# A fused attention and gated-MLP kernel: in its first pair of batches, the first layer one tile ahead and the weight sums rearranged

## The chip, the cores and the metric

The kernel runs on one core of one Trainium2 chip. Its time is device microseconds, the median of three runs. A core has a tensor engine (PE, with its weight loads as PEld), a vector engine (DVE), a scalar engine (ACT), GpSimd (POOL), and a sync engine (SP) that here only issues DMA transfers. Every engine runs its own queue strictly in order. Semaphores tie the queues together.

## The reference, cut to what matters

```python
scores = scale * x @ state^T;  a = softmax(scores);   xread = a @ state     # 512 tokens per head
scores2 = scale * state @ x^T; a2 = softmax(scores2); sread = a2 @ x        # 32 states per head
x = concat([xread, sread])           # (8 batches, 544 rows) -> 4352 rows of 512
h = x @ w_in                         # 512 -> 2048
g = h * cos(h)
out = g @ w_out                      # 2048 -> 512
```

`w_in` and `w_out` come in as float64 and are turned into float32 on the chip by integer operations. The rest is float32.

## The kernel before, in words

**Tiles and steps.** For one batch the gated layer is a grid of 16 tiles of 128 features by 512 tokens. One loop runs over `all_tiles`: a step is a tile, 16 steps are a batch, 32 (`PERIOD`) are a pair of batches; the state rows' tiles come last. Steps 0 to 27 are emitted by `first_pair`, all later ones by `later_pair`. From step 32 on tiles go two by two.

**What a tile goes through.** `hidden` (L489) is the first layer: four matmuls into a PSUM bank. `gate` (L559) on ACT rounds h to integers, `gate2` (L562) on DVE takes the difference, `gate3` (L565) on ACT is the sine, `gate4` (L579) on DVE multiplies and stores g in `g_all`. In the first pair the banks for h are two, so `hidden` of a tile waits for `gate4` of the tile two before.

**What else is in a step.** Each step of a batch has lists made by `plan`, one for each engine and place: `go(0)` is PE's work (token transposes, scores, `products`, which fold the state into `w_in`), `go(1)` ACT's copies of it ahead of `gate3`, `go(3)` DVE's part ahead of `gate4`, `go(2)`, `go(4)` and `go(5)` what comes after. Until step 16 a step also converts one block of the weights: passes 1 and 2 on ACT (L243, L246), b and c on DVE (L249, L252), the integer add d on POOL (L257). `inverse` (L383, L384) is the reciprocal of the softmax sums. At its end a step runs `first_product` or `second_product` (L632), the plain product with a11 and a12.

**The fast products.** Apart from those two, the products with `w_out` are done as seven smaller ones of an outer 2 x 2 scheme, and each of the seven again as seven stages of an inner one (`Product`, stages at L744, from step 29 on). That needs sums of weights. `weight_sum` (L1093) makes the outer sums, `inner_weights` (L670) the inner ones into four `TEMPS` and then sends eight blocks to DRAM (L672), from where `fetch_block` (L682) brings a block for each stage. `Product.sums` and `outer_sum` (both L691) are differences of g. `halves` (L508), `sw_sums` (L522) and `seven_part` (L539) do the same for the first layer from batch 2 on.

**What sets the order.** All is written out by hand. Tables tell at which step a thing is put into the queues (`weights_at`, `outer_at`, `sums_at`, `stage_at`), and memory for g is a list `quads_free` of numbered quads of `g_all`: `gate4` and `sums` take the first, and a user appends its quad when its last reader has been queued. The order in this list decides which later writer waits for which earlier reader. Quads 5 to 8 first hold `w_out` (A11, A12, A21, A22), 9 to 11 raw weights, and 4 is `TEMPS`.

Of the kernel before, what the change touches and what calls it, by code (L numbers as in the profile page):

```python
# [22 lines left out]
def kernel(  # L23
# [240 lines left out]
    class Attention:  # L264
# [117 lines left out]
        def inverse(self, v):  # L382
            nc.vector.tensor_scalar(v, v, 1e-9, None, op0=ALU.add)  # L383
            nc.vector.reciprocal(v, v)  # L384

        def sums(self):
            self.reduce1([self.z1[:, j] for j in range(2)], ALU.add)
            self.inverse(self.m1 if self.b == 0 else self.i12)

# [125 lines left out]

    def sw_sums(t, engine):
        (b11, b12, b21, b22), swS = weights_of(t)
        t1, t2, t4 = [swS[:, i] for i in range(3)]
        sub = ALU.subtract
        for o, x1, x2, op in ((t1, b21, b22, ALU.add), (t2, t1, b11, sub),  # L520
                              (t4, b12, t2, sub), (b21, b11, b21, sub)):
            engine.tensor_tensor(o, x1, x2, op=op)  # L522

# [136 lines left out]

    def inner_weights(which, m, engine=None):

        m11, m12, m21, m22 = quarters(m)
        t1, t2, t3, t4 = [quad(TEMPS)[:, n].rearrange("p (i d) -> p i d", d=P)
                          for n in range(4)]
        for o, x1, x2, op in ((t1, m21, m22, ALU.add),
                              (t2, t1, m11, ALU.subtract),
                              (t3, m11, m21, ALU.subtract),
                              (t4, m12, t2, ALU.subtract)):
            (engine or nc.gpsimd).tensor_tensor(o, x1, x2, op=op)  # L670
        for n, block in enumerate((m11, m12, t4, m22, t1, t2, t3, m21)):
            nc.sync.dma_start(  # L672
                out=blocks_kept[which, n].rearrange("p (i d) -> p i d", d=P),
                in_=block)
# [19 lines left out]
    class Product:  # L694
# [17 lines left out]
        def sums(self, k):  # L712
            lo, hi = self.quads()
            engine = nc.gpsimd
            if k == 1:
                self.q1 = quads_free.pop(0)
                self.t1 = quad(self.q1)[:, :, LO]
                self.t2 = quad(self.q1)[:, :, HI]
                sub(engine, self.t1, lo[:, :, HI], lo[:, :, LO])
            elif k == 2:  # L720
                sub(engine, self.t2, hi[:, :, HI], self.t1)
            elif k == 3:
                self.t3 = lo[:, :, HI]
                if not self.in_place:
                    self.q3 = quads_free.pop(0)
                    self.t3 = quad(self.q3)[:, :, LO]
                sub(engine, self.t3, hi[:, :, HI], lo[:, :, HI])
            else:
                sub(engine, self.t1, hi[:, :, LO], self.t2)

        def stage(self, k, copy):
# [19 lines left out]
            elif k == 2:  # L751
                nc.vector.tensor_tensor(u2, c[:, LO], t5, op=ALU.add)
                self.sums(4)
            elif k == 3:
                copy(b[:, HI], u2)  # L755
            elif k == 4:
                nc.vector.tensor_tensor(c[:, HI], c[:, LO], t5, op=ALU.add)
            elif k == 5:
                self.out(0, b)
                if self.frees:  # L760
                    quads_free.extend(quads_of[self.row][1:])
            elif k == 6:
                self.out(1, c)
                quads_free.append(self.q1)
                if not self.in_place:
                    quads_free.append(self.q3)
                if self.frees:
                    quads_free.append(quads_of[self.row][0])

# [187 lines left out]
    def plan(b):  # L957
# [3 lines left out]
        def prod(s, b, nt, *bank):  # L961
            pe[s].append((b, "products", nt) + bank)
            if b == 1 and 0 < nt < 3:
                x_dve[s].append((b, "products_taken", nt) + bank)
            else:
                x_act[s].append((b, "products_kept", nt) + bank)

# [45 lines left out]
        if b == 0:  # L1013
            pe[0].append((0, "products", 0, SIDE, HC, WC))
            y_dve[0] += [(0, "products_taken", 0, SIDE, HC, WC),
                         (0, "inverse2")]
            prod(7, 0, 2, SIDE)
            prod(11, 0, 3)
            prod(13, 1, 0, SIDE)
# [52 lines left out]
    for n in range(B // 2):  # L1072
        end = n == B // 2 - 1
        for r, engine, o, x1, x2, half in (
                ((25, 26), dve, 0, 2, 0, 0), ((27, 28), dve, 0, 2, 0, 1),
                ((28, 28), pool, 2, 3, 2, 0), ((33, 33), dve, 0, 3, 0, 0),
                ((34, 34 + (not end)), dve, 0, 3, 0, 1),
# [11 lines left out]

    def weight_sum(o, x1, x2, op):  # L1090
        for i in range(QT):
            o_, x1_, x2_ = [quad(q)[:, i:i + 1] for q in (o, x1, x2)]
            pool.tensor_tensor(o_, x1_, x2_, op=op)  # L1093

    A11, A12, A21, A22, SQ = 5, 6, 7, 8, 11
    add_, sub_ = ALU.add, ALU.subtract
    for at_, what in (
            (9, lambda: inner_weights(0, a11)),
            (13, lambda: inner_weights(1, a12)),
            (15, lambda: quads_free.append(10)),  # L1100
            (16, lambda: inner_weights(2, a22)),
            (17, lambda: quads_free.append(9)),
            (17, lambda: weight_sum(SQ, A21, A22, add_)),
            (18, lambda: inner_weights(3, matrix(SQ))),
            (19, lambda: weight_sum(A21, A11, A21, sub_)),
            (20, lambda: weight_sum(A22, SQ, A11, sub_)),
            (20, lambda: inner_weights(5, matrix(A21))),
            (22, lambda: inner_weights(4, matrix(A22))),
            (23, lambda: quads_free.append(A11)),
            (24, lambda: weight_sum(SQ, A12, A22, sub_)),  # L1110
            (25, lambda: quads_free.append(A21)),
            (25, lambda: inner_weights(6, matrix(SQ))),
            (27, lambda: quads_free.extend([A22, A12, SQ, TEMPS]))):
        weights_at[at_].append(what)
# [20 lines left out]
    def first_pair(step, t):  # L1135
        last, conv = conv_at.get(step - 1, -1), conv_at.get(step, -1)
        if step == 4:
            warm(1, acc[0])
        if step != 1:
            hidden(t)  # L1140
        if step == 0:
            hidden(all_tiles[1])
            warm(3, acc[0])
# [4 lines left out]
            go(0)  # L1148
        else:
            go(0)  # L1150
            if step == 5:
                states(1, side_banks[0])
            gate(t)
            gate2(t)
# [16 lines left out]
        if conv >= 0 and todo[1] and step > 0:  # L1171
            convert(conv, "1")
        if step == 6:
            states_kept(1, side_banks[0])
        go(2)
        if conv >= 0:
            convert(conv, "2")
        go(4)

    def later_pair(step, t, ahead):  # L1180
        coming = ahead[0] if ahead and ahead[0].paired else None
        seven_ = coming is not None and seven(coming)
        first = coming if even or coming is None else coming.mate
        if not t.paired:
            hidden(t)
        if even or not t.paired:
            gate(t)
        else:
            gate3(t.mate)
# [29 lines left out]
        go(2)  # L1219
        go(4)  # L1220

    for step, t in enumerate(all_tiles):
# [6 lines left out]
        for u in all_tiles[step + 3:step + 4]:  # L1229
            if seven(u) and u.f % 2 == 0:  # L1230
                sw_sums(u, dve if step < PERIOD else pool)
        now[0] = step
# [70 lines left out]
```

## Time and profile before

| | |
|---|---|
| time, median of 3 | 768.71 us (768.45 to 769.23) |
| span of the profiled execution | 766.2 us |
| mean granted PE clock | 0.984 |
| PE busy | 723.3 us, 94% |
| POOL, DVE, ACT busy | 526.5 us (69%), 502.0 us (66%), 328.9 us (43%) |
| HBM read, written | 87.03 MB, 23.59 MB |

The page's shares are means over stages that are unlike each other. The first pair is four stages: loads and warm-up up to about 29 us, conversion (steps 1 to 15) up to about 106, steps 16 to 27 up to about 152, and the changeover to the fast products up to about 187 us. Four fifths of the span come after that.

### The profile page before, as it was taken

What the parts mean: (1) busy time and instruction counts of PE and PEld (TensorE: products, weight loads), DVE (VectorE), ACT (ScalarE), POOL (GpSimd) and SP (SyncE); (2) the same over time, 40 slices, a digit from 0 to 9 for tenths busy, and PEclk for the clock granted to TensorE, in tenths of its full rate; (3) what the DMA queues carried; (4) which work ended last, traced back from release to release, by engine and by line L of the source; (5) the groups of instructions that cost most, each with busy time, mean ns of one, the idle gap of its engine ahead of it and who ended that gap; (6) DMA issues with size and microseconds to landing.
All of it is one profiled execution on the core that took longest, in us unless ns stands there. A gap on an engine that the chain in (4) does not pass through costs nothing.

```text
span 766.2 us, 10476 instructions
## 1 busy us (share of the span) xinstructions
PE 723.3 (94%) x3552; PEld 508.7 (66%) x3552; DVE 502.0 (66%) x691; ACT 328.9 (43%) x534; POOL 526.5 (69%) x480
## 2 busy tenths in 40 slices
PE   8998879767999999999999999999999999999998
PEld 3443323335776877677768876677778767888886
DVE  5768797876786756785965666759746447263651
ACT  3877844513444445434373446343634433211110
POOL 2344589797599875475998953759989538499610
PEclk9999999987999999999999999999999999999999
DMA  8595679478522773477225843682225446445661
GB/s 246 165 275 178 216 203 277 142 239 168 129 83 71 142 173 97 102 150 163 83 69 117 184 114 96 131 199 75 79 68 120 115 147 169 114 137 191 187 156 41
DMA packets 210356, 111.32 MB, mean 145 GB/s; under 512 B 158272, under 2 KB 173120, under 8 KB 210304
## 3 DMA queue, kind: packets, MB, share of 16 engines
q1 hardware_dynamic: 209216, 110.14, 55.3%
q8 instruction: 28, 0.46, 0.2%
q10 hardware_dynamic: 960, 0.39, 0.2%
q14 instruction: 24, 0.20, 0.1%
q0 software_dynamic: 128, 0.13, 0.1%
HBM read 87.03 MB, written 23.59 MB: 144 GB/s over the span
## 4 chain that ended last, share of the span: by engine, by line
PE 63%; POOL 19%; DVE 7%; issue 4%; ACT 3%; DMA 3%; SPq 0%; POOLq 0%; DVEq 0%; ACTq 0%
PE o L744 32%; POOL g_all L691 12%; PE h L489 11%; PE h L539 9%; PE at L328 3%; POOL g_all L670 3%; PE at L845 2%; POOL g_all L1093 2%; DMA x_b<-in_x_dram 2%; PE at L424 1%; POOL swS_all L522 1%; DVE g_all L691 1%; PE o L920 1%; DMA blocks_kept<-g_all 1%; PE o L845 1%
## 5 line engine op out<-in xcount | busy, mean ns | idle before, releaser
L691 POOL TENSOR_TENSOR g_all<-g_all 128x512 f32<-128x512 f32 x256 | 337.5, 1350 | 107.4 <-PE o L744 66.1
L744 PE MATMUL o<-g_all 128*128 128x256 f32 x1456 | 347.5, 384 | 10.3 <-DVE g_all L579 5.3
L744 PEld LDWEIGHTS o<-g_all 128*128 128x128 f32 x1456 | 275.1, 191 | 71.5 <-issue 16.8
L489 PE MATMUL h<-aT,sw 128*128 128x512 f32 x224 | 110.5, 618 | 13.9 <-DVE g_all L579 13.2
L562 DVE TENSOR_TENSOR q_all<-q_all,h 128x1024 f32<-128x1024 int32 (+1 forms) x88 | 85.4, 971 | 56.8 <-ACT q_all L559 56.6
L565 ACT ACTIVATE q_all<-q_all,halfpi 128x1024 f32<-128x1024 f32 (+1 forms) x88 | 84.2, 956 | 66.8 <-DVE q_all L562 66.8
L579 DVE TENSOR_TENSOR g_all<-h,q_all 128x1024 f32<-128x1024 f32 (+1 forms) x88 | 85.7, 974 | 36.6 <-ACT q_all L565 32.1
L559 ACT ACTIVATE q_all<-h 128x1024 int32<-128x1024 f32 (+1 forms) x88 | 73.3, 833 | 76.0 <-DVE g_all L579 33.9
L489 PEld LDWEIGHTS h<-aT,sw 128*128 128x128 f32 x224 | 41.9, 195 | 61.4 <-issue 32.9
L548 DVE TENSOR_TENSOR h<-h,sums_all 128x256 f32<-128x256 f32 x72 | 30.9, 429 | 61.9 <-PE h L539 45.2
L691 DVE TENSOR_TENSOR g_all<-g_all 128x1024 f32<-128x1024 f32 x40 | 57.9, 1463 | 0.1
L539 PE MATMUL h<-aS_all,swS_all 128*128 128x256 f32 x144 | 45.9, 401 | 6.6 <-ACT sums_all L543 5.8
L539 PE MATMUL h<-aT,sw 128*128 128x256 f32 x144 | 45.2, 396 | 3.3 <-DVE g_all L579 2.9
L749 ACT COPY o<-o 128x256 f32<-128x256 f32 x26 | 9.3, 357 | 86.5 <-PE o L744 86.5
L257 POOL TENSOR_TENSOR w_in<-w_in,aS_all 128x1024 int32<-128x1024 int32 (+1 forms) x10 | 19.3, 1927 | 37.7 <-DVE w_in L252 18.8
L539 PE MATMUL h<-aS_all,sw 128*128 128x256 f32 x144 | 43.6, 384 | 0.0
L539 PEld LDWEIGHTS h<-aS_all,swS_all 128*128 128x128 f32 x144 | 25.4, 191 | 26.2 <-issue 8.7
L670 POOL TENSOR_TENSOR g_all<-g_all 128x512 f32<-128x512 f32 x28 | 39.3, 1424 | 5.0 <-DMA blocks_kept<-g_all 4.3
L755 ACT COPY o<-sums_all 128x256 f32<-128x256 f32 x26 | 9.8, 377 | 73.6 <-PE o L744 73.5
L602 DVE SCALAR_TENSOR_TENSOR held<-o,held 128x512 f32<-128x512 f32 x40 | 27.1, 680 | 21.0 <-PE o L744 20.5
L460 ACT COPY sw<-at 128x512 f32<-128x512 f32 x50 | 26.8, 588 | 31.4 <-PE at L328 31.4
L539 PEld LDWEIGHTS h<-aT,sw 128*128 128x128 f32 x144 | 26.2, 191 | 13.0 <-DVE g_all L579 9.7
(115 smaller groups left out, 874.7 us busy)
## 6 DMA issues: line engine op xcount, KB each, us to landing
g_all<-blocks_kept SPq DMA_DIRECT2D x202, 256.0 KB, 2.8
blocks_kept<-g_all SPq DMA_DIRECT2D x56, 256.0 KB, 3.2
g_all<-in_moe_w_out_dram SPq DMA_DIRECT2D x8, 1024.0 KB, 5.1
out_dram<-ot SPq DMA_DIRECT2D x128, 64.0 KB, 2.1
g_all<-in_moe_w_in_dram SPq DMA_DIRECT2D x6, 1024.0 KB, 5.7
xT<-in_x_dram SPq DMA_DIRECT2D x96, 64.0 KB, 2.9
x_b<-in_x_dram SPq DMA_DIRECT2D x24, 256.0 KB, 4.8
x_b<-in_x_dram SPq DMA_DIRECT2D x16, 128.0 KB, 4.4
```

The lines of the kernel that those rows point to most:

```text
L460: (copy or nc.scalar.copy)(sw_of[self.b, nt][:, j, c0:c1], to[j][:, c0:c1])
L489: nc.tensor.matmul(out=t.hp, lhsT=t.lhs(i), rhs=t.rhs(i), start=(i == 0), stop=(i == t.kn - 1))
L539: nc.tensor.matmul(out=out_, lhsT=w, rhs=r, start=start, stop=True, skip_group_check=True)
L548: nc.vector.tensor_tensor(o, h2[:, LO], sums_all[:, 0], op=ALU.add)
L559: nc.scalar.activation(t.q.bitcast(I32), t.hp, func=ACTF.Copy, bias=0.25)
L562: nc.vector.tensor_tensor(t.q, t.q.bitcast(I32), t.hp, op=ALU.subtract)
L565: nc.scalar.activation(t.q, t.q, func=ACTF.Sin, bias=halfpi, scale=-TWO_PI)
L579: nc.vector.tensor_tensor(g, t.hp, t.q, op=ALU.mult)
L602: nc.vector.scalar_tensor_tensor(out=out.t[:, ch], in0=bank, scalar=TWO_PI, in1=b.t[:, ch], op0=ALU.mult, op1=ALU.add)
L670: (engine or nc.gpsimd).tensor_tensor(o, x1, x2, op=op)
L691: engine.tensor_tensor(o[:, i:i + n], x1[:, i:i + n], x2[:, i:i + n], op=ALU.subtract)
L744: nc.tensor.matmul(out=o, lhsT=ring[(self.first + k) % NB][:, i], rhs=g[:, i], start=(start and i == 0), stop=(i == QT - 1), skip_group_ch ...
```

## The change

In the first pair, `hidden` and `gate` of the next tile are put in front: a step now begins on PE with `hidden` of the step after, and ACT does `gate` of the next tile before conversion pass 2, so that a step starts with its integers ready. `states` and two `products` move one step forward to fit, and the copies of two `products` go from DVE to ACT.

The weight sums are rearranged. `inner_weights` of a11 and a12 ran in steps 9 and 13, amid the conversion; a11 now comes at step 19, and a12, first wanted in the second pair, at step 50 with temps of its own. Two of the four `weight_sum` move from POOL to DVE (steps 18 and 24), and `sw_sums` of the first pair from DVE to POOL. A pair of POOL's outer differences goes from step 28 of each pair to step 31. `Product` gives two quads back at stage 4 rather than 6, and the first product takes the second free quad rather than the first, so that tile 28 is given A21's quad. `inverse` adds its small constant through a view with the even elements first.

```diff
         def inverse(self, v):
-            nc.vector.tensor_scalar(v, v, 1e-9, None, op0=ALU.add)
+            w = v.rearrange("p (a b) -> p b a", b=2)
+            nc.vector.tensor_scalar(w, w, 1e-9, None, op0=ALU.add)
...
-    def sw_sums(t, engine):
+    def sw_sums(t):
...
-            engine.tensor_tensor(o, x1, x2, op=op)
+            nc.gpsimd.tensor_tensor(o, x1, x2, op=op)
...
-                self.q1 = quads_free.pop(0)
+                self.q1 = quads_free.pop(0 if self.n else 1)
...
             elif k == 4:
                 nc.vector.tensor_tensor(c[:, HI], c[:, LO], t5, op=ALU.add)
+                if not self.in_place:
+                    quads_free.append(self.q3)
+                if self.frees:
+                    quads_free.append(quads_of[self.row][0])
...
             elif k == 6:
                 self.out(1, c)
                 quads_free.append(self.q1)
-                if not self.in_place:
-                    quads_free.append(self.q3)
-                if self.frees:
-                    quads_free.append(quads_of[self.row][0])
...
-            if b == 1 and 0 < nt < 3:
-                x_dve[s].append((b, "products_taken", nt) + bank)
-            else:
-                x_act[s].append((b, "products_kept", nt) + bank)
+            x_act[s].append((b, "products_kept", nt) + bank)
...
-            prod(7, 0, 2, SIDE)
-            prod(11, 0, 3)
+            prod(6, 0, 2, SIDE)
+            prod(10, 0, 3)
...
-                ((28, 28), pool, 2, 3, 2, 0), ((33, 33), dve, 0, 3, 0, 0),
+                ((31, 31), pool, 2, 3, 2, 0), ((33, 33), dve, 0, 3, 0, 0),
...
+    def last_weights():
+        temps = quads_free.pop(0)
+        inner_weights(1, a12, temps)
+        weights_at[53].append(lambda: quads_free.extend([A12, temps]))
...
-            (9, lambda: inner_weights(0, a11)),
-            (13, lambda: inner_weights(1, a12)),
             (15, lambda: quads_free.append(10)),
             (16, lambda: inner_weights(2, a22)),
             (17, lambda: quads_free.append(9)),
-            (17, lambda: weight_sum(SQ, A21, A22, add_)),
+            (17, lambda: weight_sum(pool, SQ, A21, A22, add_)),
             (18, lambda: inner_weights(3, matrix(SQ))),
-            (19, lambda: weight_sum(A21, A11, A21, sub_)),
-            (20, lambda: weight_sum(A22, SQ, A11, sub_)),
-            (20, lambda: inner_weights(5, matrix(A21))),
+            (18, lambda: weight_sum(dve, A21, A11, A21, sub_)),
+            (19, lambda: inner_weights(0, a11)),
+            (20, lambda: weight_sum(pool, A22, SQ, A11, sub_)),
+            (21, lambda: inner_weights(5, matrix(A21))),
             (22, lambda: inner_weights(4, matrix(A22))),
             (23, lambda: quads_free.append(A11)),
-            (24, lambda: weight_sum(SQ, A12, A22, sub_)),
+            (24, lambda: weight_sum(dve, SQ, A12, A22, sub_)),
             (25, lambda: quads_free.append(A21)),
             (25, lambda: inner_weights(6, matrix(SQ))),
-            (27, lambda: quads_free.extend([A22, A12, SQ, TEMPS]))):
+            (27, lambda: quads_free.extend([A22, SQ, TEMPS])),
+            (50, last_weights)):
...
     def first_pair(step, t):
...
+        after = all_tiles[step + 1]
...
-            go(0)
-            if step == 5:
-                states(1, side_banks[0])
-            gate(t)
+            if step == 4:
+                warm(1, acc[0])
+                hidden(t)
+                gate(t)
+                states(1, side_banks[0])
+            if step != 3:
+                hidden(after)
+            go(0)
             gate2(t)
...
         go(2)
+        if step != 3:
+            gate(after)
         if conv >= 0:
             convert(conv, "2")
...
     def later_pair(step, t, ahead):
...
-        if not t.paired:
-            hidden(t)
-        if even or not t.paired:
+        after = all_tiles[step + 1] if step + 1 < PERIOD else t
+        if not after.paired:
+            hidden(after)
+        if t.paired and even:
             gate(t)
-        else:
+        elif t.paired:
             gate3(t.mate)
...
         go(2)
         go(4)
+        if not after.paired:
+            gate(after)
```

## What the change does to the time: the prediction

> **What bounds the kernel now.** Three views carry it. First the busy time by stretch, cut where gate4 of the tiles of steps 0, 15, 27 and 31 ends (columns: stretch, its length, then busy time and count of PE, weight load, DVE, ACT, POOL; TensorE clock; DMA share; GB/s):
>
> ```profile
> 29.20:105.80 76.60, 66.71 (x312) 28.67 (x308) 60.02 (x81) 59.88 (x84) 40.01 (x20) 0.98 0.71 225
> 105.80:152.10 46.30, 40.74 (x159) 16.53 (x160) 37.51 (x55) 22.87 (x38) 39.41 (x29) 0.96 0.76 206
> 152.10:187.40 35.30, 23.46 (x77) 14.36 (x76) 25.91 (x30) 7.25 (x15) 33.00 (x25) 0.76 0.76 194
> 187.40:766.20 578.80, 566.93 (x2905) 438.44 (x2903) 361.27 (x500) 224.21 (x376) 406.00 (x393) 1.00 0.50 124
> ```
>
> After 187 us PE is busy 98%, so whatever the first pair gains or loses is carried to the end unchanged. Before it PE is idle 9.9 + 5.6 + 11.8 = 27.3 us, and in the last stretch its clock falls to 0.76. That is the stake.
>
> Second, who waited for whom between 22 and 205 us (total, times, longest), one engine after the other:
>
> ```profile
> PE h L489 <- DVE g_all L579: 13.2, 9, 3.4
> ...
> DVE q_all L562 <- ACT q_all L559: 18.9, 15, 2.7
> ...
> ACT q_all L565 <- DVE q_all L562: 41.9, 22, 13.1
> ACT q_all L559 <- PE h L489: 17.4, 13, 6.0
> ```
>
> A ring: first layer (L489) waits for gate4 (L579, which frees its PSUM bank), gate (L559) for the first layer, gate2 (L562) for gate, gate3 (L565) for gate2. No engine is full; the ring and what is queued inside it set the step.
>
> Third, the timeline at the places where the ring is held up longest:
>
> ```profile
> 97.53 2.17 DVE L252 SCALAR_TENSOR_TENSOR g_all<-g_all 128x1024 int32<-128x1024 int32 x1
> ...
> 100.94 1.67 DVE L249 TENSOR_SCALAR g_all<-g_all 128x1024 int32<-128x1024 int32 x1
> 102.65 3.25 DVE L252 SCALAR_TENSOR_TENSOR g_all<-g_all 128x1024 int32<-128x1024 int32 x1
> ```
> ```profile
> 137.10 2.37 DVE L383 TENSOR_SCALAR i<-i 128x34 f32<-128x34 f32 x1
> ...
> 141.78 3.35 PE L489 MATMUL h<-aT,sw 128*128 128x512 f32 x4 [3.38 <-DVE g_all L579]
> ...
> 153.90 5.92 POOL L1093 TENSOR_TENSOR g_all<-g_all 128x512 f32<-128x512 f32 x4
> ...
> 160.41 0.69 DVE L579 TENSOR_TENSOR g_all<-h,q_all 128x512 f32<-128x512 f32 x1 [3.60 <-POOL g_all L1093]
> ...
> 166.31 1.35 DVE L522 TENSOR_TENSOR swS_all<-sw 128x128 f32<-128x128 f32 x1
> ...
> 172.11 0.72 ACT L565 ACTIVATE q_all<-q_all,halfpi 128x512 f32<-128x512 f32 x1 [13.09 <-DVE q_all L562]
> ```
>
> The first block: DVE's conversion instructions stretched (0.69 and 1.23 is their usual time) while POOL runs inner_weights(1). The second: the 34-element add at 2.37; gate4 of tile 28 waiting 3.60 for POOL's fourth weight sum, because tile 28 is given quad 8 that the sum still reads; then four weight differences of 1.2 to 1.35 each on DVE, and gate3 of tile 29 (L565) 13.09 late behind them. PE's stage 2 starts at 178.76, just when ACT, held up by that, has copied stage 1.
>
> [...] L383 takes 0.17 with POOL idle and ends with a POOL instruction of 1.26 otherwise (0.52, 1.02, 2.37). [...] I take 0.2, and keep 2.4 as the bad end. [...] Here four matmuls took 3.35 after 3.38 idle, against 1.88 to 1.98.
>
> **The change, part by part.** Times of one: first layer 1.73 on PE; copy, gate, gate3, one conversion pass on ACT 0.5, 0.5, 0.63, 1.04 until the next may start; gate2, gate4 0.6 and b, c 0.72, 1.14 on DVE.
>
> *One step ahead, steps 1 to 15.* DVE's waits for gate (14.9 of the 18.9 us lie here) can go, since gate of the next tile now precedes conversion pass 2. But PE gets hidden(t+1), which waits for gate4(t-1), ahead of the step's own work, and ACT copies that work before gate3(t). So in steps 4, 5, 6, 10, 12, 13 gate3 comes no sooner than 1.73 + about 1.1 + one copy after gate4 of the step before. Worked through: in step 4, hidden(4) at 43.3, states 45.0, hidden(5) 45.5, keep2 47.3, copy 48.0, gate3 48.3, gate4 49.0 against 47.0 before: +2.0. Steps 5 to 9 come out even (the copy later, the gate wait gone). Step 10: the copy of products 3 now stands before the table load: +1.0. Step 13, where PE has 5.6 us of work after hidden: +0.8. Gone: L383's 0.85 in step 10; and with inner_weights(0) and (1) out of steps 9 and 13 the stretching, (2.17 - 1.23) + (3.25 - 1.23) + (1.67 - 0.69) = 3.9 (with 0.93 for 0.69 once more, 4.1), less 0.5 because POOL's add and ACT then bind. Sum 2.0 + 1.0 + 0.8 - 0.85 - 3.6 = -0.6.
>
> *Steps 16 to 24*, from gate4(15) at 0 (before: 105.82). Step 16: the copy that DVE did beside (1.28) is on ACT behind products behind hidden(17): gate4(16) at 6.1 against 4.35, +1.7. Step 18: the sum A21 on DVE overwrites what POOL's sum SQ reads. POOL: last integer add until 5.5, inner_weights(2) 5.0, SQ 5.0, so until 15.5 (its first half until 13.0). DVE arrives at 12.1; its two halves (1.22 alone, up to 2.34 beside POOL) end at 17.5. Behind them is gate2(19), and hidden(21) waits for gate4(19): 19.0 against 12.9, +6.1. PE has hidden(20), products and second_product to do until 16.5 and idles 3. Steps 20 to 23: PE bound before, 13.35; now 13.9. Step 24: L383 2.37 to 0.2, but gate3 waits for a table load (1.28 in the trace): -1.6. Then the sum SQ on DVE, 2.5 (4.7 if POOL is busy; it waits then for its temps). Standing: +7.4 at gate4(25) to gate4(27).
>
> *POOL.* Steps 16 to 25 had 9 blocks of four at 5.0 to 6.0, ending at 60.3. Now 8, and three waits of 3.8 for temps to be stored (3.77 is such a wait in the trace): end at 58 to 59. The four differences of step 28 go behind, so t2 is ready at 64 against 70.8. POOL then waits for nobody, and nobody for it: sw_sums on POOL cost 4 x 0.46 (L522 there) and come before PE asks.
>
> *End of the pair.* Tile 28 takes quad 7, long free: of the 3.6 about 2.5 go, +5.1 at gate4(28). Without L522 on DVE 5.1 less: 0 at gate4(29), so stage 2 starts about where it did (73). But hidden(31), done before at 182.3 after stage 2 (2.2 us, slow clock), lies ahead in the idle time now: stage 3 at 76.8 against 79.6. Sum -2.8.
>
> *Second pair and later.* inner_weights(1) at step 50: 5.0 on POOL, which idles 8.4 from 285 on; its stores hold the block fetches back by about 3.5 us, three stages (3 x 3.2) before they are needed: 0, at worst 2. Quads freed at stage 4, differences at step 31 of each pair: POOL has 3.4 and 5.4 us of idle behind that place; 0.
>
> Sum -0.6 - 2.8 = -3.4: 768.7 - 3.4 = 765.3.
>
> **The rivals.** *Ahead works in full:* half of PE's 9.9 us idle in steps 1 to 15 comes back, -5: 760. For it: no engine is over 87% there. Against: the copies before gate3. *Even:* PE's idle of 3 in step 20 and of 3.9 before hidden(31) drops the clock; four matmuls at half speed, 1.7 each, eat the gain: 768.7. *Slower, DVE's sums in the ring:* both halves of A21 wait for all of SQ and take 2.34 each (+2.7), clock +1.7, the late copies cost 0.5 in each of six steps (+3): -3.4 + 7.4 = +4.0: 772.7. For it: DVE sits 5 us in front of gate2(19), on no slack in a stretch where PE had none.
>
> **How the numbers follow.** Forecast 0.40, ahead in full 0.20, even 0.15, slower 0.25. Time 765.3; range 757.5 to 773.5, from somewhat under the second case to just over the last. Faster 0.60, same 0.15, slower 0.25.
>
> **What would show it.** Right: L559 no longer waited for by L562 in steps 5 to 15; gate4(15) near 105; one gap of DVE before L691 at step 18 released by POOL L1093, and PE idle some 3 us after it; L691 on DVE twice more in 115 to 150; no wait of L579 for L1093; L522 on DVE gone; POOL's waits for blocks_kept 3 x 3.8. Wrong: gate4(15) before 101 (ahead in full) or after 108; a fetch wait of PE near step 50; POOL L691 holding PE after 187 us.

## The result and the profile after

The change makes the kernel slower: 772.80 us (771.48 to 773.41) against 768.58 us (768.43 to 769.23). The ratio is 1.0051, with a 95% interval from 1.0034 to 1.0068. The forecast was 765.3 us and faster; the time lies inside the range given, close to the rival called slower (772.7).

First the busy time by stretch of the changed kernel, with the cuts at the times of the kernel before (columns as there: stretch, length, busy time and count of PE, weight load, DVE, ACT, POOL; TensorE clock; DMA share; GB/s):

```profile
29.20:105.80 76.60, 63.59 (x300) 27.62 (x298) 54.95 (x81) 58.70 (x84) 27.61 (x13) 0.96 0.62 188
105.80:152.10 46.30, 35.68 (x126) 13.29 (x125) 32.08 (x42) 22.15 (x36) 37.60 (x27) 0.91 0.65 178
152.10:187.40 35.30, 28.97 (x121) 15.23 (x120) 25.73 (x32) 10.47 (x20) 26.05 (x22) 0.92 0.84 230
187.40:771.00 583.60, 571.38 (x2923) 441.68 (x2921) 362.50 (x503) 225.41 (x378) 419.02 (x406) 1.00 0.52 128
```

In the first stretch POOL has lost its two weight blocks (40.01 to 27.61 us), as meant, and yet PE does less in the same time: 63.59 us busy instead of 66.71. In the second it is 35.68 instead of 40.74. The third stretch gives a part back, and after 187 us PE is full, as before. So most of the loss is made before 152 us and carried to the end.

Second, who waited for whom between 22 and 205 us (total, times, longest), in the changed kernel and, in the last line, in the kernel before:

```profile
PEld h L490 <- DVE g_all L580: 44.6, 24, 5.3
ACT q_all L566 <- DVE q_all L563: 33.8, 16, 5.3
PE h L490 <- DVE g_all L580: 29.3, 15, 4.4
...
DVE g_all L580 <- ACT q_all L566: 17.4, 18, 3.0
...
DVE q_all L563 <- ACT q_all L560: 15.5, 12, 2.9
POOL g_all L671 <- DMA blocks_kept<-g_all: 11.4, 3, 3.8
ACT q_all L560 <- PE h L490: 9.9, 8, 2.6
ACT sw L461 <- PE h L328: 9.6, 6, 3.5
```
```profile
DVE g_all L579 <- ACT q_all L565: 7.4, 10, 1.3
```

The ring is still there, turned to another side. gate (L560) waits less for the first layer (L490): 9.9 instead of 17.4 us. But the first layer waits 29.3 instead of 13.2 us for gate4 (L580), and gate4 waits 17.4 instead of 7.4 us for gate3 (L566). A copy of a product (L461) now waits for PE (L328) six times, 9.6 us (twice, 1.9 us, before), and it stands in front of gate3 on ACT. gate2 (L563) still waits 15.5 us for gate, 18.9 before.

Third, the start of gate4 of some steps, read from the timeline of each kernel, as us later (+) or earlier (-) than in the kernel before, where it stands in the first row. The last column is the difference of the whole profiled span. Step 0, in front of every edit to the order, moves by -0.2 to +1.1 from one profiled execution to another, so about 1 us of a column is not the edit's.

| kernel | 0 | 15 | 18 | 19 | 27 | 29 | 31 | span |
|---|---|---|---|---|---|---|---|---|
| before (us) | 28.47 | 105.82 | 115.10 | 118.72 | 152.07 | 172.93 | 187.38 | 766.2 |
| changed | +0.91 | +2.78 | +7.44 | +10.37 | +13.35 | +4.74 | +3.34 | +4.8 |
| e1_own_first | +0.23 | -4.88 | -4.33 | +2.69 | +6.43 | -1.96 | -2.52 | -0.7 |
| e2_weights_only | -0.21 | -4.05 | -4.09 | +4.46 | +6.87 | -1.95 | -3.83 | -2.0 |
| e3_ahead_only | -0.04 | +2.82 | +6.79 | +8.97 | +11.94 | +8.18 | +9.48 | +8.8 |
| e4_sums_on_pool | +0.33 | +2.17 | +6.83 | +9.11 | +12.70 | +4.93 | +1.83 | +4.2 |
| e5_sum_later | -0.01 | -3.75 | -3.78 | -3.78 | +3.57 | -6.22 | -6.18 | -2.0 |
| e6_two_temps | -0.08 | -3.86 | -3.89 | -3.89 | +2.97 | -6.12 | -9.41 | -9.2 |
| e7_own_both | +0.89 | -3.17 | -2.62 | -2.15 | +4.32 | -4.60 | -6.22 | -4.8 |
| e8_sw_dve | +0.64 | +2.46 | +7.12 | +10.04 | +13.42 | +8.82 | +10.78 | +12.9 |
| e9_own_early | +1.14 | -3.10 | +0.73 | +4.46 | +9.14 | +0.63 | -0.77 | +1.1 |
| e10_own_late | -0.22 | +1.62 | +2.96 | +9.20 | +11.36 | +2.55 | +1.14 | +3.1 |
| e11_old_inverse | +0.18 | +3.70 | +8.35 | +11.27 | +14.54 | +5.92 | +4.52 | +5.9 |
| e12_halves | +0.15 | -3.64 | -3.67 | -3.67 | +1.72 | -6.69 | -9.56 | -8.4 |

### The profile page after: what moved, and what is told of

Same layout as the page of the kernel before. It is cut to its first block, busy times and chain, and to the rows that moved or that the text cites. A ratio compares the mean times of both kernels' runs of the same rounds, so it can differ in the third digit from the quotient of the medians.

```text
span 771.0 us, 10473 instructions
## 1 busy us (share of the span) xinstructions
PE 724.8 (94%) x3556; PEld 509.1 (66%) x3556; DVE 491.8 (64%) x683; ACT 330.5 (43%) x539; POOL 518.1 (67%) x480
## 4 chain that ended last, share of the span: by engine, by line
PE 65%; POOL 20%; DVE 5%; DMA 4%; issue 4%; ACT 2%; SPq 1%; POOLq 0%; DVEq 0%; ACTq 0%
PE o L745 31%; PE h L490 14%; POOL g_all L692 12%; PE h L540 9%; POOL g_all L671 4%; PE at L328 3%; PE at L846 2%; PE at L425 2%; POOL swS_all L523 2%; DMA blocks_kept<-g_all 1%; POOL sw L523 1%; DMA g_all<-blocks_kept 1%; PE o L921 1%; PE o L633 1%; DVE g_all L580 1%
## 5 line engine op out<-in xcount | busy, mean ns | idle before, releaser
L692 POOL TENSOR_TENSOR g_all<-g_all 128x512 f32<-128x512 f32 x256 | 337.1, 1350 | 109.8 <-PE o L745 64.4
L745 PE MATMUL o<-g_all 128*128 128x256 f32 x1456 | 343.9, 381 | 3.1 <-POOL g_all L692 2.4
L490 PE MATMUL h<-aT,sw 128*128 128x512 f32 x228 | 116.3, 636 | 30.5 <-DVE g_all L580 29.3
L563 DVE TENSOR_TENSOR q_all<-q_all,h 128x1024 f32<-128x1024 int32 (+1 forms) x88 | 85.4, 970 | 54.5 <-ACT q_all L560 53.1
L580 DVE TENSOR_TENSOR g_all<-h,q_all 128x1024 f32<-128x1024 f32 (+1 forms) x88 | 85.9, 976 | 46.1 <-ACT q_all L566 42.1
L566 ACT ACTIVATE q_all<-q_all,halfpi 128x1024 f32<-128x1024 f32 (+1 forms) x88 | 84.2, 957 | 59.4 <-DVE q_all L563 59.3
L560 ACT ACTIVATE q_all<-h 128x1024 int32<-128x1024 f32 (+1 forms) x89 | 73.9, 830 | 69.1 <-DVE g_all L580 32.3
L490 PEld LDWEIGHTS h<-aT,sw 128*128 128x128 f32 x228 | 43.0, 198 | 80.8 <-DVE g_all L580 45.1
L692 DVE TENSOR_TENSOR g_all<-g_all 128x1024 f32<-128x1024 f32 x40 | 56.9, 1438 | 0.1
L540 PE MATMUL h<-aS_all,swS_all 128*128 128x256 f32 x144 | 45.2, 396 | 2.6 <-ACT sums_all L544 1.8
L540 PE MATMUL h<-aT,sw 128*128 128x256 f32 x144 | 44.7, 392 | 3.0 <-DVE g_all L580 2.5
L671 POOL TENSOR_TENSOR g_all<-g_all 128x512 f32<-128x512 f32 x28 | 37.9, 1376 | 12.1 <-DMA blocks_kept<-g_all 11.4
L540 PE MATMUL h<-aS_all,sw 128*128 128x256 f32 x144 | 43.6, 384 | 0.0
L461 ACT COPY sw<-at 128x512 f32<-128x512 f32 x50 | 26.8, 589 | 32.9 <-PE at L328 32.9
L257 POOL TENSOR_TENSOR g_all<-g_all,aS_all 128x1024 int32<-128x1024 int32 x8 | 18.9, 2365 | 31.8 <-DVE g_all L252 28.7
L540 PEld LDWEIGHTS h<-aS_all,swS_all 128*128 128x128 f32 x144 | 25.4, 189 | 21.6 <-POOL g_all L692 7.5
```

The costliest lines, as they stand in the source:

```text
L257: nc.gpsimd.tensor_tensor(bits, bits, e, op=ALU.add)
L490: nc.tensor.matmul(out=t.hp, lhsT=t.lhs(i), rhs=t.rhs(i), start=(i == 0), stop=(i == t.kn - 1))
L540: nc.tensor.matmul(out=out_, lhsT=w, rhs=r, start=start, stop=True, skip_group_check=True)
L560: nc.scalar.activation(t.q.bitcast(I32), t.hp, func=ACTF.Copy, bias=0.25)
L563: nc.vector.tensor_tensor(t.q, t.q.bitcast(I32), t.hp, op=ALU.subtract)
L566: nc.scalar.activation(t.q, t.q, func=ACTF.Sin, bias=halfpi, scale=-TWO_PI)
```

## The experiments

### Which half of the change costs: order or weights

The changed kernel consists of an order (the next tile's first layer and gate one step ahead, all products copied by ACT) and of weights (inner weights moved, two sums on DVE, differences on POOL, quads freed earlier). Four kernels take them apart.

The order holds one more thing, which neither the description of the change nor the prediction names. At step 31 `after` is the tile itself (`else t` in `later_pair`), so its first layer and its gate, which step 30 has already put in the queues, are put in again. The changed kernel has 228 of these matmuls and 89 gates, the kernel before 224 and 88. In the changed kernel's timeline the second first layer runs with PE busy ahead of it and behind it, and gate2 of the tile waits for it:

```profile
187.26 1.88 PE L490 MATMUL h<-aT,sw 128*128 128x512 f32 x4
...
189.25 0.69 DVE L563 TENSOR_TENSOR q_all<-q_all,h 128x512 f32<-128x512 int32 x1 [1.29 <-PE h L490]
```

PE's next work starts at 188.97, so an estimate of its cost is 1.7 us. No run took it out alone. It is in every kernel below that has the new order (e1, e3, e4, e7 to e11) and in none that has the old one (e2, e5, e6, e12).

e1_own_first, the changed kernel with two lines exchanged in the first pair:

```diff
+            go(0)
             if step != 3:
                 hidden(after)
-            go(0)
```

> The changed kernel (772.8 us), with one edit in the first pair: the step's own PE work (go(0)) is issued ahead of the next tile's first layer instead of behind it. Theory A (the first layer of the next tile waits for gate4 of the step before, and what stands behind it on PE, its copies on ACT and so gate3 come late): 767 to 770 us, gate4 of step 15 back by about 2 us and gate4 of step 13 by about 3. Theory B (the loss is made by the two weight sums on DVE, which stand in front of gate2 at step 19): within 1 us of 772.8, with gate4 of step 20 still about 12 us later than in the kernel before.

Measured: 765.70 us, ratio to the kernel before 0.9962 (0.9947 to 0.9977). Theory A was right on the direction and too small: the time is 1.3 us below its interval, and gate4 of step 15 comes 7.7 us earlier than in the changed kernel, where 2 were expected. Exchanging two calls turns a kernel that is slower by 0.5% into one that is faster by 0.4%.

e2_weights_only, the changed kernel with `first_pair`, `later_pair` and the plan of products of the kernel before (the core of the edit):

```diff
-            x_act[s].append((b, "products_kept", nt) + bank)
+            if b == 1 and 0 < nt < 3:
+                x_dve[s].append((b, "products_taken", nt) + bank)
...
-            if step != 3:
-                hidden(after)
             go(0)
...
+            gate(t)
...
-        if step != 3:
-            gate(after)
```

> The changed kernel with the first pair's order, the gates' place and the plan of products of the kernel before; the moved inner weights, the two sums on DVE, the differences on POOL, step 31's outer differences and the earlier free quads stay. Theory A (the order costs): faster than both, 762 to 766 us. Theory B (the sums on DVE cost): 771 to 774. If both parts cost a half each: about 770.

Measured: 766.07 us, ratio 0.9962 (0.9945 to 0.9978): theory A, just above the upper end of its interval.

e3_ahead_only, the reverse: the kernel before with the new order and plan, and the old weights.

```diff
         else:
...
+            if step != 3:
+                hidden(after)
             go(0)
...
-            gate(t)
...
+        if step != 3:
+            gate(after)
```

> The kernel before (768.6 us) with only the order changed: next tile's first layer and gate one step ahead, all products kept by ACT, products of steps 7 and 11 one step earlier; weights as before. Theory A: 772 to 776 us, since the order costs 4 to 6 us and nothing of the weights' gain is there. Theory B: 765 to 768.

Measured: 779.04 us, ratio 1.0132 (1.0113 to 1.0150), 3 us beyond theory A's interval. So the order costs 1.32% (10 us) with the old weights, and 0.89% (7 us) with the new ones (from 0.9962 to 1.0051); some 1.7 us of each are the second first layer of tile 31, by the estimate above. The weights bring 0.4% in the old order and 0.8% in the new one.

e4_sums_on_pool, the changed kernel with both weight sums on POOL:

```diff
-            (18, lambda: weight_sum(dve, A21, A11, A21, sub_)),
+            (18, lambda: weight_sum(pool, A21, A11, A21, sub_)),
...
-            (24, lambda: weight_sum(dve, SQ, A12, A22, sub_)),
+            (24, lambda: weight_sum(pool, SQ, A12, A22, sub_)),
```

> The changed kernel with the two weight sums back on POOL, 4 instructions each at the same steps. Theory A: within 1 us of 772.8, POOL's queue longer by two blocks of 5 us, so its last block ends about 70 instead of 62 after gate4 of step 15, and some wait for it appears at step 28. Theory B: 766 to 769, and the step from gate4(18) to gate4(20) shorter by 4 us or more.

Measured: 773.87 us, ratio 1.0071 (1.0050 to 1.0092), not to be told from the changed kernel's 1.0051. The sums on DVE are not what made it slower: without them gate4 of step 19 still stands at +9.11, since in both kernels a copy in front of gate3 of step 19 waits 2.15 us for PE. At gate4 of step 27 both stand at +12.4 when step 0 is taken off.

### Where the order costs

The trace shows how the exchange of e1 acts. The timeline of the changed kernel in step 14 (start, length, engine, line, operation; in brackets the idle time before and who ended it):

```profile
98.27 1.88 PE L490 MATMUL h<-aT,sw 128*128 128x512 f32 x4
...
100.08 1.09 PE L425 MATMUL at<-x_b,xT 128*64 128x128 f32 x16
...
101.22 1.19 DVE L435 TENSOR_TENSOR sr<-at,i 32x128 f32<-32x128 f32 x4 [1.66 <-PE at L425]
...
102.42 0.69 DVE L249 TENSOR_SCALAR g_all<-g_all 128x1024 int32<-128x1024 int32 x1
...
103.15 1.23 DVE L252 SCALAR_TENSOR_TENSOR g_all<-g_all 128x1024 int32<-128x1024 int32 x1
104.41 0.69 DVE L580 TENSOR_TENSOR g_all<-h,q_all 128x512 f32<-128x512 f32 x1
...
105.15 3.78 PE L490 MATMUL h<-aT,sw 128*128 128x512 f32 x4 [3.98 <-DVE g_all L580]
```

And the same step in e1_own_first:

```profile
92.40 1.09 PE L425 MATMUL at<-x_b,xT 128*64 128x128 f32 x16
...
93.43 1.98 PE L490 MATMUL h<-aT,sw 128*128 128x512 f32 x4
93.55 1.19 DVE L435 TENSOR_TENSOR sr<-at,i 32x128 f32<-32x128 f32 x4
...
94.75 0.69 DVE L249 TENSOR_SCALAR g_all<-g_all 128x1024 int32<-128x1024 int32 x1
95.48 1.23 DVE L252 SCALAR_TENSOR_TENSOR g_all<-g_all 128x1024 int32<-128x1024 int32 x1
...
96.73 0.69 DVE L580 TENSOR_TENSOR g_all<-h,q_all 128x512 f32<-128x512 f32 x1
```

In the changed kernel the step's matmul for the totals (L425) stands behind the next first layer (L490). DVE's L435 waits 1.66 us for it, with the conversion (L249, L252) and gate4 queued behind: gate4 starts at 104.41, although gate3 had ended at 101.51 (100.77 + 0.74). The next first layer waits for that gate4, PE is idle 3.98 us, and then its four matmuls take 3.78 instead of 1.88 (granted clock 0.50 from 105.2 to 109.0). With the own work ahead, L435 waits for nobody. From this L435 to gate4 both chains are of the same length; the order moved only what stands ahead.

Two kernels say in which steps it matters. e9_own_early has the own work ahead in steps 1 to 15 alone, e10_own_late from step 16 on alone:

```diff
+            if step < 16:
+                go(0)
             if step != 3:
                 hidden(after)
-            go(0)
+            if not step < 16:
+                go(0)
```

> The changed kernel with the step's own PE work ahead of the next tile's first layer in steps 1 to 15 alone; from step 16 as in the changed kernel. If the loss of the order is made in steps 1 to 15 (gate4 of step 15 was 7.7 us earlier in the first run than in the changed kernel, and from step 15 to step 27 both lose 11): 765 to 767 us. If it is made in steps 16 to 27: 771 to 773.

> The opposite: the step's own PE work ahead in steps 16 to 27 alone. If the loss is made in steps 1 to 15: 771 to 773 us; if in steps 16 to 27: 765 to 767; with a half from each both runs give about 769.

Measured: e9_own_early 767.17 us, ratio 0.9985 (0.9976 to 0.9994), just above its interval; e10_own_late 773.20 us, ratio 1.0058 (1.0036 to 1.0081), no better than the changed kernel. The loss of the order is made in steps 1 to 15. From step 16 on the place of the own work matters little, because there the ring loses about as much in either order (gate4 of step 15 to gate4 of step 27: 10.6 us in the changed kernel, 11.3 in e1, 12.2 in e9, 9.7 in e10, against the kernel before). Up to 0.2% may lie there: e1 is at 0.9962 and e9 at 0.9985, with intervals that just touch.

### What takes the time in steps 16 to 29 instead

In e1 the wait that I had foreseen at step 18 is there. The timeline of DVE and PE in e1_own_first:

```profile
115.38 2.27 DVE L1092 TENSOR_TENSOR g_all<-g_all 128x1024 f32<-128x1024 f32 x1 [3.30 <-POOL g_all L1092]
118.80 1.23 DVE L1092 TENSOR_TENSOR g_all<-g_all 128x1024 f32<-128x1024 f32 x1 [1.15 <-POOL g_all L1092]
...
121.30 1.15 PE L328 MATMUL at<-xT,st_all 64*32 64x512 f32 x4 [3.65 <-DVE xT L310]
```

DVE stands 3.30 + 2.27 + 1.15 + 1.23 = 7.95 us in the sum A21, which waits for POOL's sum SQ, with gate2 of step 19 behind it. From gate4 of step 18 to that of step 19 e1 loses 7.0 us. In the changed kernel, where gate4 of step 18 is itself 11.8 us later, POOL is nearly done by then and the step loses 2.9. e5_sum_later takes that wait out of e2:

```diff
-            (18, lambda: weight_sum(dve, A21, A11, A21, sub_)),
...
+            (21, lambda: weight_sum(dve, A21, A11, A21, sub_)),
             (21, lambda: inner_weights(5, matrix(A21))),
```

> The kernel of the second run (new weights, old order; 766.1 us) with one edit: the weight sum A21 is put on DVE at step 21 instead of step 18, when POOL's sum SQ, which it has to wait for, is long done. Theory R (DVE's wait at step 18 holds the ring by 8 us, but POOL's queue of weight blocks sets the end of the pair): gate4 of steps 19 to 27 come about 8 us earlier than in that run, and the time stays within 1.5 us of 766. Theory S (what the ring gains is carried to the end): 758 to 760.

Measured: 767.20 us, ratio 0.9975 (0.9964 to 0.9986), against 0.9962 (0.9945 to 0.9978) of e2: no gain. That is theory R in the time; of the 8 us it expected in the ring, gate4 of step 19 came 8.2 us earlier and that of step 27 only 3.3. The span was the same. The traces point to another queue that sets the end. The first line below is from the timeline of PE in e2_weights_only, the second from its waits:

```profile
172.42 1.22 PE L540 MATMUL h<-aS_all,swS_all 128*128 128x256 f32 x2 [4.98 <-POOL swS_all L523]
```
```profile
POOL g_all L671 <- DMA blocks_kept<-g_all: 13.1, 3, 4.9
```

The second tile pair's first layer (L540) waits 4.98 us for the weight differences (L523), which are last in POOL's queue behind the inner weights (L671) and outer differences (L692); and POOL itself had stood 13.1 us waiting until the temporaries of the block ahead were stored. e6_two_temps gives two blocks other temporaries, the ring of fetched blocks, into which the first fetch is issued at step 24:

```diff
-            (18, lambda: inner_weights(3, matrix(SQ))),
+            (18, lambda: inner_weights(3, matrix(SQ), NQUAD)),
...
-            (21, lambda: inner_weights(5, matrix(A21))),
+            (21, lambda: inner_weights(5, matrix(A21), NQUAD)),
```

> As the run before it in this list, and two of the inner weight blocks (steps 18 and 21) take their four temporaries in the still unused ring of fetched blocks, so that POOL doesn't wait for the stores of the block ahead (13.1 us in three waits in the second run). Theory R: POOL's last block ends about 10 us earlier, and the time falls to 757 to 761. Theory S: no gain over the run without it, within 1 us.

Measured: 760.00 us, ratio 0.9886 (0.9866 to 0.9905). Theory R. It is faster than the kernel before and the changed one. The weight differences and the first layer behind them, in its timeline:

```profile
165.11 0.63 POOL L523 TENSOR_TENSOR swS_all<-sw 128x128 f32<-128x128 f32 x1
```
```profile
165.79 0.70 PE L540 MATMUL h<-aS_all,swS_all 128*128 128x256 f32 x2 [1.59 <-POOL swS_all L523]
```

They start at 165.11 us instead of 171.92, and PE waits 1.59 us instead of 4.98. POOL waits for stores once, 3.8 us, where e5 had three such waits, 12.6 us.

e7_own_both has the same two edits, on e1 instead of e2.

> The kernel of the first run (changed kernel with the step's own PE work ahead of the next tile's first layer; 765.7 us) with the same two edits: sum A21 on DVE at step 21, and the temporaries of steps 18 and 21 in the ring. If the order behind step 15 and the edits add: 756 to 760, a little under the run before it in this list, since gate4 of step 15 was 0.8 us earlier there. If the order of steps 16 to 24 (all products copied by ACT) costs: 2 us or more above it.

Measured: 762.57 us, ratio 0.9919 (0.9900 to 0.9937), 2.6 us above e6. In the table e7 is behind e6 by 1.0 us at step 0, 0.7 at step 15, 1.5 at step 29 and 3.2 at step 31. The last rise, 1.7 us, falls where e7 does the first layer of tile 31 a second time and e6 doesn't. So the second theory was right on the number, but not for its reason: up to step 29 the rest of the new order (gates ahead, all products copied by ACT) brings nothing and costs little. What it would bring without the second first layer was not run.

e12_halves splits the two DVE sums of e6, to see whether the gaps that they open in PE count:

```diff
-            (21, lambda: weight_sum(dve, A21, A11, A21, sub_)),
+            (20, lambda: weight_sum(dve, A21, A11, A21, sub_, slice(1))),
+            (21, lambda: weight_sum(dve, A21, A11, A21, sub_, slice(1, 2))),
...
-            (24, lambda: weight_sum(dve, SQ, A12, A22, sub_)),
+            (24, lambda: weight_sum(dve, SQ, A12, A22, sub_, slice(1))),
+            (25, lambda: weight_sum(dve, SQ, A12, A22, sub_, slice(1, 2))),
```

> The fastest so far (760.0 us) with the two DVE sums split, a half each at steps 20 and 21, 24 and 25. If the 2.5 us of a whole sum in front of gate2 open the gaps of PE (3.35 and 4.72 us, and then four matmuls at 3.6 to 3.8 instead of 1.98): 755 to 758 us. If the end of the pair is bound by POOL or the copies anyway: within 1 us of 760.

Measured: 759.98 us, ratio 0.9886 (0.9869 to 0.9903), the same as e6. gate4 of step 27 comes 1.2 us earlier and the end does not: the second theory.

### Two smaller terms of the prediction

e8_sw_dve puts the weight differences of the first pair back on DVE:

```diff
-                sw_sums(u)
+                sw_sums(u, dve if step < PERIOD else pool)
```

> The changed kernel (772.8 us) with the four weight differences of the first three-layer tile pairs in the first pair back on DVE, as in the kernel before. My prediction's term (5.1 us less on DVE ahead of gate4 of step 29): 776 to 778 us. Rival (POOL comes to these differences late, behind its last weight block, and the ring at step 27 to 29 has slack): within 1.5 us of 772.8.

Measured: 780.41 us, ratio 1.0150 (1.0132 to 1.0168), 7.6 us above the changed kernel, beyond both theories. The timeline of DVE:

```profile
176.25 1.34 DVE L523 TENSOR_TENSOR swS_all<-sw 128x128 f32<-128x128 f32 x1
177.63 1.27 DVE L523 TENSOR_TENSOR swS_all<-swS_all,sw 128x128 f32<-128x128 f32 x1
178.93 1.24 DVE L523 TENSOR_TENSOR swS_all<-sw,swS_all 128x128 f32<-128x128 f32 x1
180.09 0.28 DVE L523 TENSOR_TENSOR sw<-sw 128x128 f32<-128x128 f32 x1
...
191.77 1.19 DVE L523 TENSOR_TENSOR swS_all<-sw 128x128 f32<-128x128 f32 x1
193.00 1.24 DVE L523 TENSOR_TENSOR swS_all<-swS_all,sw 128x128 f32<-128x128 f32 x1
194.27 1.24 DVE L523 TENSOR_TENSOR swS_all<-sw,swS_all 128x128 f32<-128x128 f32 x1
195.43 1.34 DVE L523 TENSOR_TENSOR sw<-sw 128x128 f32<-128x128 f32 x1
```

The differences come twice in the first pair, for two pairs of tiles: 4.1 us in front of gate2 of step 29, and 5.0 us in front of that of step 31. I had counted the first set alone. In the table gate4 of step 29 is 4.1 us later than in the changed kernel and that of step 31 is 7.4 later.

e11_old_inverse puts the flat view back in the add of the inverse:

```diff
-            w = v.rearrange("p (a b) -> p b a", b=2)
-            nc.vector.tensor_scalar(w, w, 1e-9, None, op0=ALU.add)
+            nc.vector.tensor_scalar(v, v, 1e-9, None, op0=ALU.add)
```

> The changed kernel with the flat view back in the small add of the inverse. My prediction's terms for the new view (2.37 to 0.2 us at step 24, and 0.85 at step 10): 775 to 776 us. Rival (the view doesn't take the add out of POOL's way: it took 0.96 and 0.54 us beside POOL in the changed kernel; and DVE has slack there): within 1 us of 772.8.

Measured: 773.92 us, ratio 1.0060 (1.0037 to 1.0083), not to be told from the changed kernel's 1.0051, and nearer to the rival. The add at step 24, in the timeline of the changed kernel and then of e11_old_inverse, both while POOL computes weights:

```profile
148.18 0.96 DVE L384 TENSOR_SCALAR i<-i 128x34 f32<-128x34 f32 x1
```
```profile
149.07 1.25 DVE L383 TENSOR_SCALAR i<-i 128x34 f32<-128x34 f32 x1
```

## Why the prediction was wrong

The sum was -3.4 us and the profiled span grew by 4.8. Three terms of the sum failed: the gain on DVE in steps 1 to 15 (3.4 us), the stretch from step 16 to 27 (3.2 us), and a second first layer of tile 31 that was counted at nothing (1.7 us by an estimate). By its own steps:

**Steps 1 to 15: forecast -0.6, measured +2.8 (1.9 without what step 0 already had). This is the step that failed first, and the one that an exchange of two calls undoes.** The reason was seen: hidden of the next tile waits for gate4, and the step's own work and its copies stand behind. The rises were of the right size (forecast +2.0 up to step 4, +1.0 in step 10 and +0.8 in step 13; measured +1.8, +1.5 and +1.1). What failed is that I added to them a gain of 3.6 + 0.85 us from POOL's blocks taken away, as if the two were independent. In the old order this gain exists, and nearly in full: gate4 of step 15 stands at -4.05 in e2, by 0.8 us in step 10, 1.1 in step 14 and 1.9 in step 15. In the new order it is 1.0 us: e3, with the old weights, rises by 2.9 from step 0 to step 15 and the changed kernel by 1.9. The traces show where the other two parts went.

The 1.9 of step 15 are no gain of the weights there, because e3 has them with the old weights too. In the kernel before, the conversion pass of 3.25 us stands beside POOL's integer add (102.02 to 104.82), which inner_weights(1) had held up, and not beside inner_weights(1) itself as the prediction says. In e3 the ring is later, the add falls on the pass ahead (1.81 us), and the same pass takes 1.22. A part of the stretching never was inner_weights': in the changed kernel, too, that pass ahead takes 1.81 instead of 0.69 us (at 105.61) beside POOL's add (104.52 to 106.87). The 0.8 of step 10 were saved on DVE, where the add of the inverse takes 0.18 instead of 1.02, and were lost again in the wait of gate4 for gate3, which stands behind a copy and a table load on ACT (1.28 us at 81.80 in the changed kernel). The first line is from e3, the second from the changed kernel:

```profile
82.87 0.69 DVE L579 TENSOR_TENSOR g_all<-h,q_all 128x512 f32<-128x512 f32 x1 [1.37 <-ACT q_all L565]
```
```profile
83.84 0.69 DVE L580 TENSOR_TENSOR g_all<-h,q_all 128x512 f32<-128x512 f32 x1 [2.21 <-ACT q_all L566]
```

Time won on DVE is worth nothing where DVE then waits for another engine.

**Steps 16 to 27: forecast +7.4 more, measured +10.6.** gate4 of step 19 was forecast at +6.1 from gate4 of step 15, 1.7 of it in step 16 and 4.4 behind the sum A21. It came at +7.6: 3.1 in step 16, where the copies stand in front of gate3 as foreseen, 1.6 in step 18 and 2.9 in step 19. The 2.9 are for the most part not the sum's, since e4 loses 2.3 there without it; e1 shows the sum at 7.0 where the ring is early. So I had the wait right, and its place in this kernel wrong. The 1.6 of step 18 are those of a slow first layer (granted clock 0.50 from 117.1 to 120.4), for whose end gate waits:

```profile
116.78 3.55 PE L490 MATMUL h<-aT,sw 128*128 128x512 f32 x4 [2.58 <-DVE g_all L580]
...
120.43 0.60 ACT L560 ACTIVATE q_all<-h 128x512 int32<-128x512 f32 x1 [2.35 <-PE h L490]
```

Steps 20 to 24 came nearly as forecast in sum (-1.0, measured -0.7). Step 25 was forecast at about +2.5 for the sum SQ on DVE and lost 2.5, but that was luck: e4, without this sum, loses 2.8 there. In both, gate3 stands behind a copy (L413) that waits for PE's transposes (L408), which stand behind the next tile's first layer; in the changed kernel the granted clock was 0.50 there (151.3 to 154.6). The first two lines are from the changed kernel, the third from e4:

```profile
151.45 3.54 PE L490 MATMUL h<-aT,sw 128*128 128x512 f32 x4 [4.39 <-DVE g_all L580]
...
155.46 0.59 ACT L413 COPY xT<-at 128x512 f32<-128x512 f32 x1 [4.44 <-PE at L408]
```
```profile
154.26 0.59 ACT L413 COPY xT<-at 128x512 f32<-128x512 f32 x1 [4.50 <-PE at L408]
```

What was left out of the sum, and stood only in the rivals, is the clock. These two first layers take about 1.6 us more than usual each; the kernel before had one such layer in this stretch (1.4 more, at 141.78, granted clock 0.50 from 142.3 to 145.6). A third stands just ahead of the stretch (105.15, 1.9 more). How much of the 3.2 us by which the sum is short is the clock's is argued from the trace: no run took the clock alone away. One pair of executions shows what a slow layer costs. e11 and the changed kernel do the same up to step 11, where the add of the inverse takes 0.18 us in both, and come to the same first layer after the same gap, the changed kernel first:

```profile
84.59 1.98 PE L490 MATMUL h<-aT,sw 128*128 128x512 f32 x4 [2.06 <-DVE g_all L580]
```
```profile
83.84 3.32 PE L489 MATMUL h<-aT,sw 128*128 128x512 f32 x4 [2.06 <-DVE g_all L579]
```

With step 0 taken off, the two are equal at gate4 of step 11; at that of step 12 e11 is 1.65 us later, and it still is at step 15.

**POOL:** right in its waits (three of 3.8; 11.4 us in all) and wrong in what they are worth. "POOL then waits for nobody, and nobody for it" holds only because the ring is late. With the old order and A21 later it isn't, and POOL's queue sets the end of the pair (e5): taking two of the three waits out is then worth 0.9% (e5 to e6, 0.9975 to 0.9886).

**End of the pair: forecast to give back 10.2 us, measured 8.9** (from +13.35 at gate4 of step 27 to +4.5 at stage 3: 189.95 against 185.46 us). The cause was right: no wait for POOL's fourth sum at tile 28, and no differences on DVE. The differences were priced at 5.1 and are worth 7.6 (e8), since they come twice. hidden(31) lies in the idle time as foreseen, but at a granted clock of 0.50 (178.6 to 181.8): 3.68 us, after a gap of 3.76. And it is done once more behind stage 2 (187.26), where PE has no idle time. The sum had this second first layer at nothing. Without its 1.7 us the pair would have given back 10.6 by this estimate, near the 10.2 of the forecast.

**Second pair and later: forecast 0, at worst 2.** From step 33 until the state rows' tiles at the end the shift of gate4 stays between 4.4 and 5.2 us. The one new wait is the fetch that the stores of step 50 hold back: 0.74 us.

```profile
300.08 1.97 PE L745 MATMUL o<-g_all 128*128 128x256 f32 x8 [0.74 <-DMA g_all<-blocks_kept]
```

**The signs named beforehand:** two more sums on DVE, L522 off DVE, no wait of gate4 of tile 28 for a weight sum, and three waits of 3.8 came as said (the sums show as L1092, the line of the instruction itself). DVE's gap at step 18 was 1.17 us and PE's behind it 1.28, where about 3 was forecast, because the ring came late. gate2's wait for gate did not go in steps 5 to 15. And "gate4(15) after 108", named as a sign of error, is what came: 108.60.

**The rivals:** the one called slower was right on the time (772.7), and right that copies in front of gate3 and the clock (0.50 granted in four of the first layers) would eat the gain; its main cause, DVE's sums in the ring, is refuted by e4, and it doesn't have the second first layer, so that its number was right by luck. "Ahead works in full" is refuted in steps 1 to 15, where PE was to win half of its idle time and is busy 3.1 us less.

## What to carry to other kernels

A saving on one engine and a new order of the queues are not to be added: first follow which engine the critical chain runs through in the new order, and count the saving only where that engine is still the one waited for. Work issued ahead should go behind the work of the current step when it waits for the end of the step before, since everything issued after it waits too (here gate4 of step 14, 2.9 us behind the end of gate3). When a gap is closed and nothing is gained, look for the next queue that ends at the same place: here a second set of temporaries was worth more than the whole change was forecast to bring. After moving work to another step of a loop, count the instructions of both kernels: four matmuls and one gate more were the sign that the last step of the pair did its tile again.

## What the runs showed of the hardware

In the traces of both kernels every engine's instructions start in the order of the program: in the changed kernel 681 on DVE, 507 on ACT, 470 on POOL (fills and table loads left out), SP's 564 transfers, and PE's 3556 matmuls line by line. So in step 14, when L435 waits 1.66 us, L249, L252 and gate4 start behind it.

Strided or flat, the 34-element add stays in POOL's way: with POOL at work it took 0.96 us in the new view (148.18 in the changed kernel) and 1.25 in the old (149.07 in e11_old_inverse). With POOL idle it took 0.18 in the new view (81.05 in the changed kernel) and 0.17 in the old (310.07 in the kernel before). In these two kernels it ran beside POOL nine times, in 0.48 to 2.37 us, and ended each time 0.04 to 0.05 us after an instruction of POOL; at 148.18 it ended at 149.14, POOL's L671 at 149.10. In e2_weights_only, in the new view, it took 0.27 (143.67); where POOL stood there is not shown. The 0.2 that the prediction took for step 24 in the new view was its author's estimate.

The length of the last gap alone doesn't tell whether PE comes back at half speed. Four matmuls took 3.55 us after 2.58 idle (116.78 in the changed kernel, granted clock 0.50 from 117.1 to 120.4), 2.95 after 2.07 (97.48 in e1_own_first), but 1.98 after 2.06 (84.59 in the changed kernel, granted clock 1.00 from 84.6 to 86.6). Even the same first layer behind the same work and the same gap of 2.06 took 1.98 in the changed kernel and 3.32 in e11_old_inverse. In the kernel before, the granted clock was 0.50 behind each gap of over 2 us: 2.93 us up to 100.48 (0.50 from 101.4 to 104.7), 3.38 up to 141.78 (142.3 to 145.6), 5.30 up to 161.23 (161.2 to 166.0), 3.90 and 2.64 up to 174.05 and 178.76 (174.0 to 183.0). What decides the cases near 2 us is not shown by these runs.
